# Halving additions for the pooled keys and values, and one minimum per chunk moved to GpSimd

## The chip, the cores and the metric

The kernel runs on one core of a Trainium2 chip. The time is the device time of one execution in microseconds (us); the figure for a kernel is the median of several runs. The engines are called here as the profile calls them: PE (TensorE), DVE (VectorE), ACT (ScalarE), POOL (GpSimd) and SP (SyncE, whose queue issues the transfers).

## The reference, cut to what matters

Attention over keys and values that are averaged in groups of eight rows, then two MLPs one after the other. All data is float32.

```python
def _attn_ref(q, k, v):                     # (8, 8, 576, 64): batch, heads, rows, depth
    k_p = k.reshape(B, H, 72, 8, D).mean(axis=3)
    v_p = v.reshape(B, H, 72, 8, D).mean(axis=3)
    scores = np.matmul(q, k_p.transpose(0, 1, 3, 2)) / np.sqrt(D)
    ...                                     # softmax over the 72 pooled rows
    return np.matmul(attn, v_p)             # regrouped to x: 4608 tokens x 512

def _moe_ref(x, w_in, w_out):               # 512 -> 2048 -> 512
    h = x @ w_in
    g = np.where(h >= 1, h, np.where(h <= -1, 0.0, (h + 1) ** 2 / 4))
    return g @ w_out

def _moe2_ref(x, w_in, w_out):              # 512 -> 2048 -> 512
    h = x @ w_in
    return (h / (1 + np.exp(-h))) @ w_out
```

## The kernel before, in words

The 4608 tokens are worked in 9 tiles of 512 tokens for each MLP. A tile has 16 chunks of 128 hidden features, so the main loop runs over steps `s`, sixteen to a tile. Precision is kept by splitting every float32 operand into two float16 halves, a high and a low one, so that each product takes three matmuls (`three`, lines 116 to 118).

**A step of the first MLP.** `emit_h(s)` issues 12 matmuls into a PSUM bank called `hps` (two such banks take turns from tile 1 on). Then, for the chunk of the step before, ACT computes `u = relu(scale * h + bias)` out of that bank (`pre_A`, line 747), the minimum of `u` with one is taken (`min_A`, which calls the helper `ts`, line 89), ACT squares it (`mid_A`, line 753), and DVE takes the maximum with the scaled `h`, once more out of the bank (`post_A`, line 762). Only when `post_A` is through is the bank free for `emit_h` of two steps later. ACT and DVE then split the result into two halves (`split_g`, lines 815 and 816), and three steps after `emit_h` its 12 matmuls into the output banks `y` follow (`emit_yA`). Tile 0 runs apart from the others: its minimum is with two, and its second matmuls wait until the weights have been converted.

**Attention** is worked beside that, 128 tokens at a time, one or two "slots" a step: scores (PE), maximum and difference (DVE, lines 503 and 504), exponential (ACT, 508), sum and reciprocal (DVE, 523 to 527), normalisation (POOL, line 528, into `e`), halves of it (ACT 533, POOL 534), a transposing transfer, and the product with the values (PE, 582), whose result is split into `xh` and `xl` (line 322), the input of the next tile.

**Pooling keys and values** is `kv_pool`. A piece is two heads of one batch: a tile `raw` of 72 partitions that holds, for each head, 8 rows of 64 numbers. There are 8 batches x (keys, values) x 4 pieces = 64. Of these, 12 (values of batch 0, keys and values of batch 1) are pooled on POOL by three halving additions (lines 385 and 386), and 52 on DVE by one `tensor_reduce` that reads the eight rows with a stride (line 388). From batch 2 on the eight pieces of a batch are pooled close together, once in about 100 us.

**Weights** are converted from float32 in between (ACT 169, 203 and 204; DVE 177, 91, 189 and 195; POOL 205).

The order of the instructions on each engine is written down by the program's own scheduler at build time, from the order of the code and its priorities; on the chip each engine then works its list strictly in that order.

Of the kernel before, what the change touches and what calls it, by code (L numbers as in the profile page):

```python
# [13 lines left out]
ALU = mybir.AluOpType  # L14
AX = mybir.AxisListType
# [18 lines left out]
def tile_pooled_attention_two_mlps(  # L34
# [18 lines left out]
    nc = tc.nc  # L53
# [8 lines left out]
    KF = DFF // 128  # L62
# [9 lines left out]
    ON_POOL = [(0, "v"), (1, "k"), (1, "v")]  # L72
# [14 lines left out]
    def ts(out, in0, s1, s2=None, op0=ALU.mult, op1=None):  # L87
        if op1 is None:
            nc.vector.tensor_scalar(out=out, in0=in0, scalar1=s1, scalar2=None, op0=op0)  # L89
        else:  # L90
            nc.vector.tensor_scalar(out=out, in0=in0, scalar1=s1, scalar2=s2, op0=op0, op1=op1)
# [283 lines left out]
    def kv_pool(b, which, hp):  # L375

        if hp == 0:
            sums[b, which] = kvp.tile([SPT, H, D], F32, tag="sum", name="sum", bufs=3)
            if which == "k":
                nc.gpsimd.memset(sums[b, which][SP // 32 * 32:SPT], 0.0)  # L380
        dst = sums[b, which][0:SP, 2 * hp:2 * hp + 2]
        r = kv_raw.pop((b, which, hp))
        if (b, which) in ON_POOL:
            for n in (4, 2):
                nc.gpsimd.tensor_tensor(out=r[:, :, 0:n], in0=r[:, :, 0:n], in1=r[:, :, n:2 * n], op=ALU.add)
            nc.gpsimd.tensor_tensor(out=dst, in0=r[:, :, 0], in1=r[:, :, 1], op=ALU.add)
        else:
            nc.vector.tensor_reduce(out=dst, in_=r.rearrange("p h r d -> p h d r"), axis=AX.X, op=ALU.add)  # L388

# [333 lines left out]
    g_t, h_t, u_t, g32_t = {}, {}, {}, {}  # L725
# [21 lines left out]
            nc.scalar.activation(out=u, in_=h_t[s], func=AF.Relu, scale=c_A(r, "ch", s), bias=0.5)  # L747

    def min_A(s, r):
        ts(u_t[s], u_t[s], 2.0 if s < KF else 1.0, op0=ALU.min)  # L750

    def mid_A(s, r):
        nc.scalar.activation(out=u_t[s], in_=u_t[s], func=AF.Square, scale=0.5 if s < KF else r["rsg"])  # L753
# [161 lines left out]
    def pool_to(n):  # L915
        while done["pool"] < min(n, len(kv)):
            load_to(done["pool"] + 4)
            x = kv[done["pool"]]
            if done["pool"] >= 16:
                paced(lambda: kv_pool(*x))  # L920
            else:
                kv_pool(*x)
            done["pool"] += 1
# [28 lines left out]
    r = XT[0]  # L952
# [11 lines left out]
    for s in range(KF + 1):  # L964
        if s < KF:
            while n1 < min(len(cuts1), piece_of(cuts1, s) + 2):
                convert1(n1)
                n1 += 1
            emit_h(s, chunk1, r["x"])
        z = s - 1  # L970
        if z >= 0:
            pre_A(z, r)
            min_A(z, r)
            mid_A(z, r)
            post_A(z, r)
# [38 lines left out]
    for s in range(KF, LAST + LAG):  # L1014
# [4 lines left out]
        if KF <= z < LAST:  # L1019
            if z < NTILE * KF:  # L1020
                pre_A(z, XT[z // KF])
                min_A(z, XT[z // KF])
            else:
                act_B(z, XT[z // KF])
# [75 lines left out]
```

## Time and profile before

| | |
|---|---|
| Median of 3 runs | 1745.93 us (1745.43 to 1748.97) |
| The profiled execution, whole | 1752.34 us |
| Its span, first to last instruction | 1750.4 us |
| Mean granted PE clock in it | 0.961 of full speed |
| PE busy in the span | 1620.5 us (93%) |
| DVE busy | 904.8 us (52%) |
| ACT busy | 776.8 us (44%) |
| POOL busy | 220.7 us (13%) |

Matmuls are pipelined, so a share of busy time on PE says that it had work, not that it ran at its peak. The work changes along the span: loading, the first attention tiles and tile 0 until about 230 us; tiles 1 to 8 of the first MLP, with attention beside them until about 870 us; the end of the first MLP until 990 us and then the second MLP. The averages above run over all of these.

### The profile page before, as it was taken

How to read it: one execution, taken by the hardware profiler on the slowest of the kernel's cores; microseconds unless marked ns; L12 is line 12 of the kernel's file. 1: busy time of each engine (PE TensorE's matmuls, PEld its weight loads, DVE VectorE, ACT ScalarE, POOL GpSimd, SP SyncE). 2: the span in 40 equal slices, each digit the busy share in tenths (PEclk: the TensorE clock that was granted, in tenths of full speed). 3: DMA queues.
4: the chain of work that ended last, by engine and by line, in shares of the span. 5: the costliest groups of instructions: out<-in, count | busy, mean ns of one | idle time of the engine just before them, and what ended most of it. 6: DMA issues, size and time to landing. Idle time of an engine off the chain costs nothing.

```text
span 1750.4 us, 21833 instructions
## 1 busy us (share of the span) xinstructions
PE 1620.5 (93%) x8594; PEld 757.5 (43%) x8594; DVE 904.8 (52%) x1714; ACT 776.8 (44%) x1215; POOL 220.7 (13%) x195
## 2 busy tenths in 40 slices
PE   4763789999998999999999999999999999999998
PEld 3321334444444444444444444444444444444443
DVE  8797778878788597886535331212121312122111
ACT  3575455665646556475434433333332323233232
POOL 5733412121221112112100000000000000000000
PEclk8786789999999999999999999999999999999999
DMA  9414655655659346342241010000000000000000
GB/s 283 127 57 119 138 130 128 149 127 125 154 125 269 89 131 148 90 120 61 55 187 49 10 63 25 25 25 24 25 25 25 25 24 25 25 25 25 0 25 24
DMA packets 206086, 144.55 MB, mean 83 GB/s; under 512 B 153120, under 2 KB 170528, under 8 KB 204832
## 3 DMA queue, kind: packets, MB, share of 16 engines
q1 hardware_dynamic: 205984, 143.16, 30.8%
q8 instruction: 67, 1.10, 0.3%
q14 instruction: 35, 0.29, 0.0%
HBM read 88.08 MB, written 27.26 MB: 66 GB/s over the span
## 4 chain that ended last, share of the span: by engine, by line
PE 64%; DVE 18%; ACT 7%; DMA 6%; issue 2%; POOL 1%; SPq 0%; ACTq 0%; POOLq 0%; DVEq 0%
PE hps L116 10%; PE hps L118 10%; PE hps L117 10%; PE y L863 7%; PE y L862 7%; PE y L861 7%; DVE sum L388 5%; PE y L116 3%; PE y L118 3%; PE y L117 3%; DVE g L816 2%; DVE g L762 2%; DMA raw<-in_moe_w_in_dram 1%; DVE xf L189 1%; DVE xf L195 1%
## 5 line engine op out<-in xcount | busy, mean ns | idle before, releaser
L819 DVE SCALAR_TENSOR_TENSOR g<-g,tsg,g 128x512 f16<-128x512 f32 x144 | 108.2, 751 | 479.6 <-ACT g L818 478.5
L808 ACT ACTIVATE g<-hps,tc 128x512 f32<-128x512 f32 x144 | 99.0, 687 | 504.7 <-PE hps L118 502.1
L116 PE MATMUL hps<-xh,wa 128*128 128x512 f16 x576 | 226.3, 393 | 40.0 <-DVE g L762 22.7
L117 PE MATMUL hps<-xl,wa 128*128 128x512 f16 x576 | 226.2, 393 | 0.0
L118 PE MATMUL hps<-xh,wa 128*128 128x512 f16 x576 | 224.3, 391 | 1.8 <-POOL wa L205 1.8
L116 PE MATMUL hps<-xh,wch 128*128 128x512 f16 x576 | 218.3, 379 | 0.0
L117 PE MATMUL hps<-xl,wch 128*128 128x512 f16 x576 | 218.3, 379 | 0.0
L118 PE MATMUL hps<-xh,wcl 128*128 128x512 f16 x576 | 218.3, 379 | 0.0
L861 PE MATMUL y<-wdh,g 128*128 128x512 f16 x576 | 218.3, 379 | 0.0
L862 PE MATMUL y<-wdl,g 128*128 128x512 f16 x576 | 218.3, 379 | 0.0
L863 PE MATMUL y<-wdh,g 128*128 128x512 f16 x576 | 218.3, 379 | 0.0
L117 PE MATMUL y<-g,wb 128*128 128x512 f16 x544 | 206.9, 380 | 2.3 <-DVE g L816 1.7
L118 PE MATMUL y<-g,wb 128*128 128x512 f16 x544 | 206.8, 380 | 0.0
L116 PE MATMUL y<-g,wb 128*128 128x512 f16 x544 | 203.5, 382 | 0.4 <-ACT y L849 0.4
L753 ACT ACTIVATE u<-u,trsg 128x512 f32<-128x512 f32 x128 | 91.9, 719 | 87.7 <-DVE u L89 87.7
L762 DVE SCALAR_TENSOR_TENSOR g<-hps,tc,u 128x512 f32<-128x512 f32 x136 | 101.5, 746 | 54.8 <-ACT u L753 53.8
L816 DVE TENSOR_TENSOR g<-g,g 128x512 f16<-128x512 f32 x128 | 97.2, 760 | 50.6 <-ACT g L815 49.1
L747 ACT ACTIVATE u<-hps,tch 128x512 f32<-128x512 f32 x128 | 87.0, 680 | 72.6 <-PE hps L118 72.3
L815 ACT CAST g<-g 128x512 f16<-128x512 f32 x128 | 78.5, 614 | 83.4 <-DVE g L762 81.0
L89 DVE TENSOR_SCALAR u<-u 128x512 f32<-128x512 f32 x144 | 75.8, 526 | 66.5 <-ACT u L747 66.1
L818 ACT ACTIVATE g<-g,tsg 128x512 f16<-128x512 f32 x144 | 103.8, 721 | 4.5
L117 PEld LDWEIGHTS <-wa 128*128 128x128 f16 x576 | 57.9, 101 | 96.1 <-issue 37.3
(171 smaller groups left out, 2047.2 us busy)
## 6 DMA issues: line engine op xcount, KB each, us to landing
raw<-in_moe_w_out_dram SPq DMA_DIRECT2D x24, 1024.0 KB
raw<-in_moe_w_in_dram SPq DMA_DIRECT2D x10, 1024.0 KB
raw<-in_k_dram SPq DMA_DIRECT2D x32, 288.0 KB
raw<-in_v_dram SPq DMA_DIRECT2D x32, 288.0 KB
y<-y SPq DMA_DIRECT2D x36, 256.0 KB
yin<-y SPq DMA_DIRECT2D x9, 1024.0 KB
out_dram<-osb SPq DMA_DIRECT2D x36, 256.0 KB
qt<-in_q_dram SPq DMA_DIRECT2D x32, 256.0 KB
```

Source lines behind the costliest of these rows:

```text
L116: nc.tensor.matmul(out=acc, lhsT=wh, rhs=xh, start=start, stop=False)
L117: nc.tensor.matmul(out=acc, lhsT=wh, rhs=xl, start=False, stop=False)
L118: nc.tensor.matmul(out=acc, lhsT=wl, rhs=xh, start=False, stop=stop)
L753: nc.scalar.activation(out=u_t[s], in_=u_t[s], func=AF.Square, scale=0.5 if s < KF else r["rsg"])
L762: return nc.vector.scalar_tensor_tensor(out=g, in0=h_t.pop(s), scalar=c_A(r, "c1", s), in1=u_t.pop(s), op0=ALU.mult, op1=ALU.max)
L808: nc.scalar.activation(out=g, in_=ps, func=AF.Silu, scale=r["c1"][:, p:p + 1])
L816: return nc.vector.tensor_tensor(out=gl, in0=g, in1=gh, op=ALU.subtract)
L818: nc.scalar.activation(out=gh, in_=g, func=AF.Copy, scale=r["sg"])
L819: nc.vector.scalar_tensor_tensor(out=gl, in0=g, scalar=r["sg"], in1=gh, op0=ALU.mult, op1=ALU.subtract)
L861: nc.tensor.matmul(out=a, lhsT=h_, rhs=w[0][:, m], start=st, stop=False)
L862: nc.tensor.matmul(out=a, lhsT=h_, rhs=w[1][:, m], start=False, stop=False)
L863: nc.tensor.matmul(out=a, lhsT=l_, rhs=w[0][:, m], start=False, stop=sp)
```

## The change

The reduction on DVE is replaced by the three halving additions that POOL already used for its 12 pieces: rows 0 to 3 plus rows 4 to 7 (512 numbers a partition), rows 0 and 1 plus rows 2 and 3 (256), row 0 plus row 1 (128). And the minimum of tiles 1 to 8 (`s >= KF`, 128 of the 144) is issued on POOL; tile 0 keeps it on DVE. The line numbers after line 384 shift by one or two (762 becomes 761, 528 becomes 526, 816 becomes 815, 534 becomes 532).

```diff
         dst = sums[b, which][0:SP, 2 * hp:2 * hp + 2]
         r = kv_raw.pop((b, which, hp))
-        if (b, which) in ON_POOL:
-            for n in (4, 2):
-                nc.gpsimd.tensor_tensor(out=r[:, :, 0:n], in0=r[:, :, 0:n], in1=r[:, :, n:2 * n], op=ALU.add)
-            nc.gpsimd.tensor_tensor(out=dst, in0=r[:, :, 0], in1=r[:, :, 1], op=ALU.add)
-        else:
-            nc.vector.tensor_reduce(out=dst, in_=r.rearrange("p h r d -> p h d r"), axis=AX.X, op=ALU.add)
+        e = nc.gpsimd if (b, which) in ON_POOL else nc.vector
+        for n in (4, 2):
+            e.tensor_tensor(out=r[:, :, 0:n], in0=r[:, :, 0:n], in1=r[:, :, n:2 * n], op=ALU.add)
+        e.tensor_tensor(out=dst, in0=r[:, :, 0], in1=r[:, :, 1], op=ALU.add)

     def min_A(s, r):
-        ts(u_t[s], u_t[s], 2.0 if s < KF else 1.0, op0=ALU.min)
+        e = nc.vector if s < KF else nc.gpsimd
+        e.tensor_scalar(out=u_t[s], in0=u_t[s], scalar1=2.0 if s < KF else 1.0, scalar2=None, op0=ALU.min)
```

Since the scheduler writes the order anew, many instructions change places. On DVE, this is the place in tile 1 where the eight pieces of batch 2 are pooled. Before (L388 the reductions, L89 the minimum, L762 `post_A`, L816 the split, L322 the attention output, L195 a weight conversion):

```order
L89 TENSOR_SCALAR u<-u 128x512
L524 TENSOR_SCALAR den<-den 128x8
L527 RECIPROCAL den<-den 128x8
L388 TENSOR_REDUCE sum<-raw 72x128 x4
L762 SCALAR_TENSOR_TENSOR g_2580<-hps,tc_1316,u 128x512
L388 TENSOR_REDUCE sum<-raw 72x128
L104 TENSOR_REDUCE wg<-all 128x1
L322 SCALAR_TENSOR_TENSOR xl<-att,tsv,xh 128x4x128
L388 TENSOR_REDUCE sum<-raw 72x128
L89 TENSOR_SCALAR u<-u 128x512
L816 TENSOR_TENSOR g_2636<-g_2580,g_2636 128x512
```

The same place in the changed kernel, from its first addition on (L385 and L386 the additions, L761 `post_A`, L815 the split, L189 a weight conversion):

```order
L385 TENSOR_TENSOR raw<-raw 72x2x256 x4
L385 TENSOR_TENSOR raw<-raw 72x2x128
L761 SCALAR_TENSOR_TENSOR g_2502<-hps,tc_1324,u 128x512
L385 TENSOR_TENSOR raw<-raw 72x2x128 x3
L386 TENSOR_TENSOR sum<-raw 72x128 x3
L815 TENSOR_TENSOR g_2616<-g_2502,g_2616 128x512
L189 SCALAR_TENSOR_TENSOR xf<-raw,xf 128x1024
L386 TENSOR_TENSOR sum<-raw 72x128
L104 TENSOR_REDUCE wg<-all 128x1
L322 SCALAR_TENSOR_TENSOR xl<-att,tsv,xh 128x4x128
L761 SCALAR_TENSOR_TENSOR g_2620<-hps,tc_1324,u 128x512
```

The pieces are still taken four together, but as additions of four different pieces in turn, with a `post_A` among them, and the minimum is gone from the list.

On POOL, this is the end of tile 0 and the begin of tile 1, before (L205 weight conversion, L528 the normalisation, L534 its halves):

```order
L205 TENSOR_TENSOR wb_124<-xf,wb_124 128x1024 x2
L528 TENSOR_TENSOR e<-e,den 128x576
L534 TENSOR_TENSOR e_113<-e,e_113 128x4x72
L534 TENSOR_TENSOR e_114<-e,e_114 128x4x72
L528 TENSOR_TENSOR e<-e,den 128x576
L534 TENSOR_TENSOR e_113<-e,e_113 128x4x72
L534 TENSOR_TENSOR e_114<-e,e_114 128x4x72
L205 TENSOR_TENSOR hl<-xf,hl 128x1024
```

And the same place in the changed kernel (L749 the minimum, L526 the normalisation, L532 its halves):

```order
L205 TENSOR_TENSOR wb_124<-xf,wb_124 128x1024 x2
L749 TENSOR_SCALAR u<-u 128x512 x4
L526 TENSOR_TENSOR e<-e,den 128x576
L532 TENSOR_TENSOR e_113<-e,e_113 128x4x72
L532 TENSOR_TENSOR e_114<-e,e_114 128x4x72
L749 TENSOR_SCALAR u<-u 128x512
L526 TENSOR_TENSOR e<-e,den 128x576
L749 TENSOR_SCALAR u<-u 128x512
L532 TENSOR_TENSOR e_113<-e,e_113 128x4x72
L532 TENSOR_TENSOR e_114<-e,e_114 128x4x72
L749 TENSOR_SCALAR u<-u 128x512
L205 TENSOR_TENSOR hl<-xf,hl 128x1024
```

The minima now stand between the attention's and the conversion's instructions in POOL's one list, so each waits until those ahead of it are through.

## Rows read from the trace of the kernel before

**Rows 1.** The page, parts 1 and 2: busy times, and PE's granted clock in 40 slices.

```profile
PE 1620.5 (93%) x8594; PEld 757.5 (43%) x8594; DVE 904.8 (52%) x1714; ACT 776.8 (44%) x1215; POOL 220.7 (13%) x195
...
PEclk8786789999999999999999999999999999999999
```

**Rows 2.** Busy time by stretch: start, length, each engine's busy time, clock, DMA share, GB/s.

```profile
230.00:870.00 640.00, 608.03 (x3789) 288.21 (x3789) 499.80 (x982) 370.30 (x620) 119.51 (x106) 0.98 0.52 126
300.00:320.00 20.00, 15.20 (x62) 6.31 (x61) 16.59 (x23) 9.34 (x15) 0.09 (x1) 0.91 0.74 188
...
720.00:740.00 20.00, 17.33 (x95) 8.16 (x95) 19.27 (x19) 8.45 (x16) 4.85 (x4) 1.00 0.44 115
870.00:1750.00 880.00, 875.67 (x4086) 398.82 (x4084) 225.18 (x390) 286.81 (x418) 0.00 (x0) 1.00 0.09 34
```

**Rows 3.** Waits of PE from 230 to 870 us: total, times, longest.

```profile
PE hps L116 <- DVE g L762: 22.7, 15, 3.8
```

**Rows 4.** DVE in order of time, the pooling of batch 2: start, length, instruction.

```profile
294.85 7.38 DVE L388 TENSOR_REDUCE sum<-raw 72x128 f32<-72x1024 f32 x4
302.13 0.75 DVE L762 SCALAR_TENSOR_TENSOR g<-hps,tc,u 128x512 f32<-128x512 f32 x1
302.79 1.92 DVE L388 TENSOR_REDUCE sum<-raw 72x128 f32<-72x1024 f32 x1
...
307.29 0.43 DVE L89 TENSOR_SCALAR u<-u 128x512 f32<-128x512 f32 x1
```

**Rows 5.** ACT in order of time, same place; idle time before in brackets.

```profile
302.26 0.63 ACT L393 ACTIVATE rows<-sum 80x512 f32<-80x512 f32 x1 [4.66 <-DVE sum L388]
...
307.75 0.72 ACT L753 ACTIVATE u<-u,trsg 128x512 f32<-128x512 f32 x1 [3.68 <-DVE u L89]
```

**Rows 6.** PE in order of time, same place.

```profile
313.75 0.38 PE L116 MATMUL hps<-xh,wa 128*128 128x512 f16 x1 [3.06 <-DVE g L762]
```

**Rows 7.** Waits of PE from 125 to 230 us.

```profile
PE att L582 <- DVE xl L322: 7.3, 1, 7.3
```

**Rows 8.** DVE's and ACT's instructions by line: count, ns min/median/max.

```profile
L388 DVE TENSOR_REDUCE sum<-raw x52: 1842/1904/1955, 4.4 to 735.4; 72x128 f32<-72x1024 f32 x52
L816 DVE TENSOR_TENSOR g<-g,g x128: 640/692/2204, 241.8 to 991.1; 128x512 f16<-128x512 f32 x128
L189 DVE SCALAR_TENSOR_TENSOR xf<-raw,xf x26: 1208/1219/2065, 18.4 to 806.7; 128x1024 int32<-128x1024 int32 x26
L89 DVE TENSOR_SCALAR u<-u x144: 373/420/2071, 67.5 to 988.4; 128x512 f32<-128x512 f32 x144
L762 DVE SCALAR_TENSOR_TENSOR g<-hps,tc,u x136: 694/750/753, 70.9 to 989.7; 128x512 f32<-128x512 f32 x136
L747 ACT ACTIVATE u<-hps,tch x128: 662/682/700, 237.0 to 987.7; 128x512 f32<-128x512 f32 x128
L753 ACT ACTIVATE u<-u,trsg x128: 703/722/727, 238.8 to 988.9; 128x512 f32<-128x512 f32 x128
```

**Rows 9.** POOL's instructions by line.

```profile
L380 POOL MEMSET sum<- x8: 517/518/687, 3.2 to 625.8; 16x512 f32 x8
L801 POOL TENSOR_TENSOR stash<-g,stash x2: 1155/1156/1157, 123.5 to 125.1; 128x512 f16<-128x512 f32 x2
L205 POOL TENSOR_TENSOR hl<-xf,hl x16: 2124/2131/3163, 275.2 to 815.5; 128x1024 f16<-128x1024 f32 x16
L528 POOL TENSOR_TENSOR e<-e,den x36: 1144/1150/1600, 31.2 to 860.4; 128x576 f32<-128x576 f32 x36
L534 POOL TENSOR_TENSOR e<-e,e x64: 722/732/1987, 179.6 to 863.2; 128x288 f16<-128x288 f32 x64
```

**Rows 10.** DVE in order of time, one split.

```profile
474.88 2.20 DVE L816 TENSOR_TENSOR g<-g,g 128x512 f16<-128x512 f32 x1 [1.88 <-ACT g L815]
```

**Rows 11.** POOL in order of time, same moment.

```profile
474.41 2.13 POOL L205 TENSOR_TENSOR hl<-xf,hl 128x1024 f16<-128x1024 f32 x1 [5.67 <-ACT hl L204]
```

**Rows 12.** Waits of POOL from 230 to 870 us.

```profile
POOL e L528 <- DVE den L527: 278.7, 22, 31.6
```

## The prediction, made before the changed kernel was run

> **What bounds the kernel now.** The page comes first: PE is busy for 1620.5 of 1750.4 us, and the granted clock is below nine tenths only in the first six of 40 slices, some 260 us [rows 1]. The busy time by stretch then says where PE lacks work. From 870 us to the end it is busy 875.67 of 880 us with 4086 matmuls, one per 0.214 us: nothing in that half is to be won [rows 2]. From 230 to 870 us it idles 640 - 608.03 = 32.0 us, while DVE is busy for 499.8 us (78%) and POOL for 119.5 (19%) [rows 2]. PE's waits name the releaser: 22.7 us, in 15 waits, are an `hps` bank that `post_A` on DVE has not yet freed [rows 3]. PE is the bound there, and a late DVE is what interrupts it.
>
> The timeline shows how. At 294.85 us DVE begins the pooling of batch 2 with four reductions in one run, 7.38 us [rows 4]. ACT, next to read a sum, stands 4.66 us; then the minimum of the following chunk lies behind more reductions until 307.29, and ACT's square waits 3.68 us for it [rows 5]. At the end PE waits 3.06 us for the bank [rows 6]. There are five such places (300, 400, 500, 620 and 720 us); the first leaves PE idle for 4.80 us of 20, the last 2.67 [rows 2], and with the three between (2.31, 1.57, 3.80) that is 15.2 us, half of the 32.0.
>
> **How much lateness a chunk bears.** Between the end of `emit_h(s)` and the start of `emit_h(s+2)` in the same bank PE does 36 other matmuls: 36 x 0.214 = 7.7 us [rows 2]. In that time ACT 0.68, the minimum 0.42, ACT 0.72 and DVE 0.75 must run, 2.57 us [rows 8]. So 5.1 us are left for queueing. A run of 7.38 us overdraws it by 2.3; PE's waits of up to 3.8 us [rows 3] are of that size.
>
> **The change, part by part.**
>
> *The sums.* 52 reductions of 1.90 us go [rows 8]; next to each other they take 7.38 / 4 = 1.85 us each [rows 4]. Additions of two SBUF operands on DVE are seen at 512 elements (692 ns) and, in the weight conversion, at 1024 (1219 ns) [rows 8]: 1.03 ns an element and 165 ns fixed, so 428 ns at 256 and 297 at 128. The three add up to 1.42 us if each waits for the one before: the worst price, which saves 0.43. The list, though, takes the same step of four pieces in a row, and neighbours overlap: the reductions take 1.90 alone and 1.85 in a row. The real overlap of short instructions is not in these rows; taking 0.08 us off each gives 1.18 us a piece and saves 0.67. I take 0.6. For 52 pieces that is 31 us of DVE's time (22 to 35). A run of four becomes 4 x 1.25 = 5.0 us, just below the 5.1 us that a chunk bears, and it is cut by a `post_A`.
>
> *The minimum.* 128 instructions of 0.42 us leave DVE, 54 us more. POOL has no one-input arithmetic of this size in the trace. Its memset of the same 512 elements takes 0.52 us, its two-input operation 1.16 [rows 9]; these are the bounds, and since one stream is read instead of none or two I take 0.8. The chain of a chunk becomes 0.68 + 0.8 + 0.72 + 0.75 = 2.95 us, 0.4 longer, and 4.75 us of slack are left. In tiles 7 and 8 this is hidden entirely: PE runs without a gap there, and POOL has nothing else to do.
>
> *What the minimum queues behind.* POOL does 64 halves of 0.73 us, 36 normalisations of 1.15 and 16 conversions of 2.13 [rows 9]. Running, none of them alone uses up 4.75 us. Standing, they might: a normalisation at the head of POOL's list has waited for DVE 278.7 us in 22 times [rows 12]. What is behind it now is a minimum, which ACT's square waits for, then `post_A`, then PE. That mean of 12.7 us is mostly POOL arriving early with nothing to do before; now it has a minimum in that time, so I expect waits of 1 to 3 us.
>
> *The port.* A split that DVE began at 474.88, 0.47 us after a POOL conversion, took 2.20 us instead of 0.69, and ended when POOL did [rows 10, 11]. The same line has a median of 692 ns and a maximum of 2204; the reduction lies between 1842 and 1955 always, and `post_A`, with one operand in PSUM, between 694 and 753 [rows 8]. So the change exchanges instructions that POOL cannot stretch for 156 that it can, and gives POOL 128 x 0.8 = 102 us more to run. The Trainium skill has this as a rule: SBUF — State Buffer, "Who interferes with whom", says that a DVE instruction with two SBUF inputs contends with a GpSimd instruction that reads SBUF, that the second to start blocks fully, and that `tensor_reduce` never contends. By that rule, the rows above agreeing, both halves of the change get in each other's way. Price: from 230 to 870 us some 105 of the 128 minima make POOL busy for 84 us more, 13% of the time; about 320 DVE instructions with two SBUF operands or of the `u` kind then meet it with that chance and lose about half of 0.8 us: 320 x 0.13 x 0.4 = 17 us of DVE's time. It takes back a fifth of the 85 us freed.
>
> *The sum, in PE's time.* Before 125 us: one run of four sums, -1. 125 to 230 us: PE waits 7.3 us for an attention result that stands behind eight sums [rows 7]; 8 x 0.6 is 4.8, of which I count -3, because weight conversions stand between them. The five places: of 15.2 us two thirds, -10 (0 to -15). The other 16.8 us of idle time from 230 to 870, partly of transfers: a quarter, as DVE loses a tenth of its load and the minimum no longer queues there, -4. The clock is at 0.91 in the first of the five places [rows 2]; fewer gaps there give -2. Contention and the longer chain: +4. Together -16 us. Against the profiled execution's 1752.34 us that is 1736; the median of the runs shown is 6.4 us below that execution, so it is 1745.93 - 16 = 1730 us.
>
> **The rivals.**
>
> *A, slower: the minimum is stuck in POOL's list.* From 230 to 870 us there are about 28 attention rounds, and each has a normalisation that waits for DVE. If POOL stands at one for over 4.75 us with a minimum behind it, PE stops. If one round in three does so by 3.5 us, that is 9 x 3.5 = 32 us against a gain of 16: 1762. For it: POOL's longest wait was 31.6 us [rows 12]. Against it: the list is ordered by when things should be ready, and DVE, the one waited for, is the engine that is relieved.
>
> *B, hidden.* The five places lose their reductions, but the next wait ends as late (ACT's head also waits for transfers), and only the -1 and -3 before 230 us stay: 1742.
>
> *C, the port takes it all.* If POOL's minimum is 1.16 us and additions in a row meet it each time, the 17 us become 50 or more and the runs of additions are as long as the reductions were: 1747. This also is the case in which the additions are no cheaper than what they replace.
>
> *D, everything goes.* All 32.0 us of idle time save some 3 of transfers, 4 before 230 us, and half of the 2% that the clock lacks from 230 to 870 us (0.98 [rows 2], 12.8 us): 29 + 4 + 7 = 40, so 1706. For it: 22.7 of the 32.0 us have one cause [rows 3].
>
> **How the numbers follow.** Forecast 0.52, A 0.12, B 0.14, C 0.12, D 0.10. A measurement of this kernel tells 0.2%, 3.5 us, from no change. The forecast and D are faster, and half of B, which ends at that bound: 0.69. Same: the other half of B and most of C: 0.17. Slower: A and the rest of C: 0.14. The range leaves out A and part of D, and takes in B, C and the bounds of the sums: 1712 to 1750; the forecast's own range is 1720 to 1738.
>
> **What would show it.** Right: runs of four pieces on DVE at 4.7 to 5.7 us; PE's wait for `post_A` from 230 to 870 us down from 22.7 to below 12; the minimum on POOL at 0.6 to 1.0 us when alone; ACT's square seldom waiting over 2 us for it; PE's busy time after 870 us unchanged. Wrong: additions of 512 often above 1.2 us (C); ACT's square waiting over 5 us for POOL, with POOL idle at a normalisation just ahead (A); PE's idle time unchanged with transfers as releasers (B). Also, the new order on every engine may bring stalls of its own, which no row of before can show.

## The result, and the profile after

The changed kernel takes 1764.16 us (median of 4 runs, 1763.76 to 1766.61), the kernel before 1745.68 us (4 runs): a ratio of 1.0104, 95% interval 1.0087 to 1.0122. It is 18 us slower, where 16 us faster was forecast, and it lies outside the range of 1712 to 1750 us.

The page of the changed kernel, part 1:

```profile
PE 1615.4 (92%) x8594; PEld 754.8 (43%) x8594; DVE 848.9 (48%) x1690; ACT 778.4 (44%) x1215; POOL 444.1 (25%) x323
```

DVE was relieved, but by less than planned: 904.8 us busy before [rows 1], 848.9 now, 56 us less, where the forecast freed 85 and gave 17 of them back to the port. POOL's busy time doubled, from 220.7 to 444.1 us. The 128 minima alone keep it busy for 218 of these 223 us more, where the forecast had 102. The granted clock is where it was (a mean of 0.964, before 0.961).

The busy time by stretch of the changed kernel (columns as in [rows 2]):

```profile
230.00:870.00 640.00, 592.90 (x3692) 280.55 (x3692) 450.84 (x953) 365.51 (x608) 299.75 (x205) 0.99 0.53 127
870.00:1760.00 890.00, 890.00 (x4187) 405.78 (x4183) 222.72 (x380) 294.74 (x430) 41.55 (x29) 1.00 0.09 33
```

PE's idle time from 230 to 870 us is 640 - 592.90 = 47.1 us, against 32.0 [rows 2]: 15 us more, about the 14.3 us by which the two profiled executions differ (1766.61 against 1752.34). After 870 us PE never waits, as before (the 4.3 us that [rows 2] lacks there lie behind its last matmul). So the loss lies in the stretch where attention runs beside the MLP, and DVE with 49 us less to do there (450.84 against 499.80) did not help.

What each engine waited for from 230 to 870 us in the changed kernel (total, times, longest); PE:

```profile
PE hps L116 <- DVE g L761: 23.7, 19, 3.1
PE y L117 <- DVE g L815: 7.1, 4, 3.3
PE all L103 <- ACT rows L391: 5.0, 2, 2.9
```

DVE:

```profile
DVE g L761 <- ACT u L752: 87.8, 44, 4.8
...
DVE raw L385 <- DMA raw<-in_v_dram: 18.1, 12, 3.4
```

ACT:

```profile
ACT g L814 <- DVE g L761: 84.5, 66, 8.0
ACT u L752 <- POOL u L749: 82.9, 59, 3.1
```

POOL:

```profile
POOL u L749 <- ACT u L745: 205.9, 62, 11.8
POOL e L526 <- DVE den L525: 47.7, 19, 4.5
```

The bank that waits for `post_A` costs PE 23.7 us, where it cost 22.7 [rows 3]. So only 1 of the 15 us is at the bank; the rest is spread over waits that were 2.8 us or less before, the split (7.1) and the attention's rows (5.0) first. ACT's square stands 82.9 us for the minimum on POOL, in small pieces. And there is a wait that was not foreseen: DVE, at the first of a piece's additions, stands for the load of the values.

The same two links of the chain in the kernel before:

```profile
ACT u L753 <- DVE u L89: 75.2, 57, 3.7
```

```profile
DVE g L762 <- ACT u L753: 37.3, 38, 3.1
```

The square stood nearly as long for a minimum that was late on DVE as it now stands for one that is long on POOL. And `post_A` stands 50 us more for the square (87.8 against 37.3), as much as DVE was relieved of: the freed time is spent waiting in the same chain. Such a wait of DVE is not by itself a loss of PE's: in the kernel without a minimum, shown further down, it is 94.8 us.

### The profile page after: what moved, and what is told of

The parts are those of the page before. It is cut to its first block, busy times and chain, and to the rows that moved or that the text cites. A ratio compares the mean times of both kernels' runs of the same rounds, so it can differ in the third digit from the quotient of the medians.

```text
span 1764.8 us, 21992 instructions
## 1 busy us (share of the span) xinstructions
PE 1615.4 (92%) x8594; PEld 754.8 (43%) x8594; DVE 848.9 (48%) x1690; ACT 778.4 (44%) x1215; POOL 444.1 (25%) x323
## 4 chain that ended last, share of the span: by engine, by line
PE 60%; DVE 15%; DMA 9%; ACT 7%; POOL 4%; issue 4%; SPq 1%; DVEq 0%; POOLq 0%; ACTq 0%
PE hps L117 10%; PE hps L116 10%; PE hps L118 10%; PE y L862 7%; PE y L861 7%; PE y L860 7%; PE y L116 3%; PE y L118 3%; DMA raw<-in_v_dram 3%; PE y L117 3%; POOL u L749 2%; DVE raw L385 2%; DMA qT<-rows 2%; DVE g L761 2%; DVE xf L195 1%
## 5 line engine op out<-in xcount | busy, mean ns | idle before, releaser
L749 POOL TENSOR_SCALAR u<-u 128x512 f32<-128x512 f32 x128 | 218.2, 1705 | 318.5 <-ACT u L745 296.7
L116 PE MATMUL hps<-xh,wa 128*128 128x512 f16 x576 | 224.4, 390 | 36.2 <-DVE g L761 23.7
L118 PE MATMUL hps<-xh,wa 128*128 128x512 f16 x576 | 221.1, 386 | 3.4 <-POOL wa L205 3.4
L761 DVE SCALAR_TENSOR_TENSOR g<-hps,tc,u 128x512 f32<-128x512 f32 x136 | 101.4, 745 | 152.8 <-ACT u L752 152.4
L815 DVE TENSOR_TENSOR g<-g,g 128x512 f16<-128x512 f32 x128 | 102.9, 804 | 50.1 <-ACT g L814 48.8
```

The costliest lines, as they stand in the source:

```text
L116: nc.tensor.matmul(out=acc, lhsT=wh, rhs=xh, start=start, stop=False)
L118: nc.tensor.matmul(out=acc, lhsT=wl, rhs=xh, start=False, stop=stop)
L749: e.tensor_scalar(out=u_t[s], in0=u_t[s], scalar1=2.0 if s < KF else 1.0, scalar2=None, op0=ALU.min)
L761: return nc.vector.scalar_tensor_tensor(out=g, in0=h_t.pop(s), scalar=c_A(r, "c1", s), in1=u_t.pop(s), op0=ALU.mult, op1=ALU.max)
L815: return nc.vector.tensor_tensor(out=gl, in0=g, in1=gh, op=ALU.subtract)
```

## The experiments

Nine kernels were timed, five rounds each, against the kernel before. A difference in us below is the ratio less 1, times 1748 us, the median of before in those runs; a ratio's interval of about 0.0013 either way is some 2 us.

### One half of the change at a time

The sums alone (the minimum back on DVE):

```diff
-        e = nc.vector if s < KF else nc.gpsimd
-        e.tensor_scalar(out=u_t[s], in0=u_t[s], scalar1=2.0 if s < KF else 1.0, scalar2=None, op0=ALU.min)
+        ts(u_t[s], u_t[s], 2.0 if s < KF else 1.0, op0=ALU.min)
```

> Halving additions on DVE, the minimum stays on DVE. M (the minimum on GpSimd is the cost: 1.49 us instead of 0.42 in every chunk's chain): without it the sums bring what was forecast, -5 to -15 us against before, 1731 to 1741. S (the sums are the cost: taken four pieces in turn they hold all four raw buffers, and DVE stands at the next addition until a late value load lands, 18 us of such waits after the change): +8 to +18, 1754 to 1764, with the same waits of additions for value loads in the profile. P (only the two together cost, by the shared port): -8 to 0, and 512-element additions near 0.69 us instead of 0.90.

Measured: 1.0033 [1.0019, 1.0046], 5.8 us slower. That is in none of the three ranges; S has the sign and comes nearest. P is out: it had 0.69 us for the additions of 512, and their mean is 0.87. These additions of 512, by line and shape (busy us, mean ns of one, idle time before them and its releasers):

```profile
L385 DVE TENSOR_TENSOR raw<-raw 72x512 f32<-72x512 f32 x52 | 44.0, 874 | 21.7 <-DMA raw<-in_v_dram 17.0 <-DMA raw<-in_k_dram 4.7
```

The minimum alone (the reduction back on DVE, the minimum on POOL):

```diff
-        e = nc.gpsimd if (b, which) in ON_POOL else nc.vector
...
+        else:
+            nc.vector.tensor_reduce(out=dst, in_=r.rearrange("p h r d -> p h d r"), axis=AX.X, op=ALU.add)
```

> The minimum of tiles 1 to 8 on GpSimd, the reductions stay. M: most of the loss, +12 to +20 us against before, 1758 to 1766. S: no loss, -5 to +3, 1741 to 1749, since reductions free their buffer one by one. P: -5 to +3 as well, and the minimum near its 1.49 us with few longer ones, because reductions do not take the port.

Measured: 1.0074 [1.006, 1.0088], 12.9 us slower, as M said. The minimum in it, by line (ns minimum, median, maximum), and as a group (busy us, mean ns of one, idle time before):

```profile
L751 POOL TENSOR_SCALAR u<-u x128: 1474/1484/3177, 237.4 to 998.0; 128x512 f32<-128x512 f32 x128
```

```profile
L751 POOL TENSOR_SCALAR u<-u 128x512 f32<-128x512 f32 x128 | 210.7, 1647 | 347.0 <-ACT u L747 328.0 <-DVE sq L91 11.2 <-DVE xl L322 4.4
```

Each half loses by itself, and 5.8 + 12.9 = 18.7 us is, within the intervals, the 18.2 us that both lose together: each half has a cost of its own.

### The sums: the order of the additions

In the changed kernel the additions stand four pieces at a time: four first steps, four second, four third. A piece's `raw` buffer, of which there are four, comes free only with its last step. Here the three additions of a piece are tied behind the last addition of the piece before; first with the minimum on POOL, then with the minimum on DVE:

```diff
+    pooled = []
...
-        for n in (4, 2):
-            e.tensor_tensor(...)
-        e.tensor_tensor(out=dst, in0=r[:, :, 0], in1=r[:, :, 1], op=ALU.add)
+        with tc.issue_after(pooled[-1].ins) if pooled and e is nc.vector else nullcontext():
+            for n in (4, 2):
+                e.tensor_tensor(...)
+            y = e.tensor_tensor(out=dst, in0=r[:, :, 0], in1=r[:, :, 1], op=ALU.add)
+        if e is nc.vector:
+            pooled.append(y)
```

> The whole change, but on DVE the three additions of a piece are queued behind the last addition of the piece before, so that a raw buffer comes free after each piece. S: the waits of additions for value loads fall from 18 us to under 5, and the time to 1745 to 1752. M: the waits fall too, but the time stays at 1758 or above. P: as M.

Measured: 1.0045 [1.0031, 1.0059], 7.9 us slower instead of 18.2. That lies between the range of S and that of M: the order costs 10 us of the whole change, and the rest stays.

> Halving additions on DVE, each piece queued behind the one before, and the minimum on DVE. If the order of the additions was the whole cost of the sums (with it changed, the whole change lost 10 us of its 18), the cheaper sums now bring a gain: -3 to -8 us against before, 1741 to 1746. If the sums cost something else too (the port, more instructions), 0 to +5, 1749 to 1754.

Measured: 0.9945 [0.9929, 0.9962], 9.6 us **faster** than before; it beats both kernels, and by more than the first expectation allowed. The minimum's move, added to it, costs 17.5 us (from -9.6 to +7.9), where it costs 12.9 with the reductions; the difference is at the edge of what the intervals tell. DVE in order of time in the changed kernel, at the pooling of a batch (start, length, instruction):

```profile
405.83 3.39 DVE L385 TENSOR_TENSOR raw<-raw 72x512 f32<-72x512 f32 x4
...
409.27 1.82 DVE L385 TENSOR_TENSOR raw<-raw 72x256 f32<-72x256 f32 x4
411.02 1.96 DVE L386 TENSOR_TENSOR sum<-raw 72x128 f32<-72x128 f32 x4
412.91 0.74 DVE L761 SCALAR_TENSOR_TENSOR g<-hps,tc,u 128x512 f32<-128x512 f32 x1
417.06 0.69 DVE L385 TENSOR_TENSOR raw<-raw 72x512 f32<-72x512 f32 x1 [3.42 <-DMA raw<-in_v_dram]
```

And at the same work in the kernel with the sums in turn and the minimum on DVE:

```profile
415.20 0.27 DVE L388 TENSOR_TENSOR sum<-raw 72x128 f32<-72x128 f32 x1
415.40 0.67 DVE L387 TENSOR_TENSOR raw<-raw 72x512 f32<-72x512 f32 x1
416.00 0.73 DVE L764 SCALAR_TENSOR_TENSOR g<-hps,tc,u 128x512 f32<-128x512 f32 x1
416.66 0.40 DVE L387 TENSOR_TENSOR raw<-raw 72x256 f32<-72x256 f32 x1
417.10 0.29 DVE L388 TENSOR_TENSOR sum<-raw 72x128 f32<-72x128 f32 x1
417.31 0.68 DVE L387 TENSOR_TENSOR raw<-raw 72x512 f32<-72x512 f32 x1
```

The chain of work that ended last, of the changed kernel, behind this run of four (start, length, what):

```profile
413.25 3.71 DMA raw<-in_v_dram
```

In the changed kernel, four pieces take 405.83 to 412.98, 7.1 us, as long as the reductions' 7.38 [rows 4]. No `raw` buffer comes free before the last steps, which begin at 411.02; so a load of values starts at 413.25, takes 3.71 us, and at 417.06 DVE has stood 3.42 us for it. In the kernel with the sums in turn a piece's steps are sprinkled between the chunks' instructions, a buffer comes free with each third step, and the first step seldom waits. The groups by line and shape of that kernel, and its waits of PE from 230 to 870 us:

```profile
L387 DVE TENSOR_TENSOR raw<-raw 72x512 f32<-72x512 f32 x52 | 36.2, 697 | 7.8 <-DMA raw<-in_v_dram 4.5 <-DMA raw<-in_k_dram 3.1
...
L387 DVE TENSOR_TENSOR raw<-raw 72x256 f32<-72x256 f32 x52 | 32.8, 631 | 0.4
L388 DVE TENSOR_TENSOR sum<-raw 72x128 f32<-72x128 f32 x52 | 20.5, 394 | 1.1
```

```profile
PE hps L116 <- DVE g L764: 4.6, 5, 2.1
```

DVE's idle time at the loads fell from 21.7 us (sums alone) to 7.8, and PE's wait for the bank to 4.6. The additions themselves did not get cheaper: 36.2 + 32.8 + 20.5 = 89.5 us busy, against 87.4 with the sums alone (44.0, and 28.1 and 15.3 for the shorter two). The edit does two things at once, it frees buffers sooner and it breaks the long run into instructions of some 0.3 to 0.7 us with others between; which of them gives how much of the 15 us is open. Additions four in turn with more buffers would tell; this was not tried. Nor was the run of reductions broken up with other instructions between, which would tell whether the gain needs additions at all.

### The minimum: its time, its place, or the port

Half of the columns on POOL (the reductions on DVE; the minimum of columns 256 to 511 is left out):

```diff
+            h = u_t[s][:, 0:N // 2]
+            nc.gpsimd.tensor_scalar(out=h, in0=h, scalar1=1.0, scalar2=None, op0=ALU.min)
```

> As the kernel with the minimum alone on GpSimd, but the minimum is taken of the first 256 of the 512 columns only; the other half of it is left out. M: the instruction takes some 0.75 to 0.8 us, and at least half of the loss of the full-width one is gone, 1746 to 1755. S and P: no difference to the full-width one beyond 4 us, as it was no loss.

Measured: 1.0018 [1.0007, 1.0029], 3.1 us slower: three quarters of the loss are gone, as M said. Next, two that separate DVE's relief from POOL's link, again with the reductions on DVE. The first leaves out the minimum of tiles 1 to 8 on every engine. The second puts three memsets of `u` in its place, which write as many elements and read none (the values of `u` are left out):

```diff
         if s < KF:
             ts(u_t[s], u_t[s], 2.0, op0=ALU.min)
+        else:
+            for i in range(3):
+                nc.gpsimd.memset(u_t[s], 0.5)
```

> The kernel before with the minimum of tiles 1 to 8 left out on every engine. This is what the relief of DVE is worth by itself, with nothing in its place on GpSimd and a shorter chain. Forecast's step (a late DVE is what stops PE): -8 to -20 us, 1729 to 1741, and PE's waits for the bank from 230 to 870 us under 15. If PE's waits have other causes: -5 to 0.

Measured without a minimum: 0.9911 [0.9896, 0.9927], 15.6 us faster. Its busy time by stretch:

```profile
230.00:870.00 640.00, 618.07 (x3896) 294.96 (x3896) 454.60 (x884) 379.12 (x629) 116.83 (x106) 0.99 0.55 133
```

PE's idle time there is 21.9 us, against 32.0: a DVE relieved of the minimum, in a chain that is shorter by it, is worth about what the forecast hoped for, so long as nothing takes the minimum's place.

> The minimum of tiles 1 to 8 replaced by three GpSimd memsets of the same tile, so the minimum and the values of u are left out; GpSimd is as long in the chain (3 x 0.52 us) and as busy, but reads nothing from SBUF. L (the length of the chain is the cost): as with the minimum on GpSimd, +8 to +14 us, 1757 to 1763. P (the port is the cost): the split on DVE is never stretched by it, and the time falls to 1740 to 1749.

Measured with three memsets: 1.0044 [1.0031, 1.0058], 7.7 us slower, so 23 us above the kernel without a minimum, with the same relief of DVE. L holds (its range began at +8, which the interval takes in), and P does not. To see whether the length of the link counts, or the two hand-overs between ACT and POOL, the loop was cut to one memset, as here, and to two:

```diff
-            for i in range(3):
+            for i in range(1):
```

> The reductions stay on DVE; in place of the minimum of tiles 1 to 8 GpSimd writes a constant over the chunk once (the values are left out). DVE is relieved of 0.42 us a chunk as in the changed kernel, and the link in the chain is one memset, 0.52 us. If the length of the link on GpSimd is what costs, with no price for the hand-over itself, the time lies on the line through the kernel without a minimum (-15.5 us, link of 0) and that with three memsets (+7.7 us, 1.59 us): -8 us. If the two hand-overs between ACT and GpSimd cost most of it whatever the length, it lies close to the kernels with a longer link: 0 to +4 us. If relief of DVE is worth nothing by itself and only the shorter chain paid in the kernel without a minimum, it equals the kernel before or is a little slower, 0 to +3, and two memsets a step more.

> As with one memset, but two in a row on GpSimd, a link of 1.05 us. If the length of the link is what costs: on the line between no link and three memsets, 0 us (-15.5 + 23.2 x 1.05 / 1.59 = -0.2). If the hand-over costs and not the length: within 2 us of both one and three memsets, +4 to +8. Against it stands the minimum over half of the columns, a link of 0.84 us that also reads SBUF, at +3: if reading costs by itself, this kernel is no slower than that one though its link is longer.

Measured: one memset 0.9944 [0.993, 0.9958], 9.8 us faster; two 1.0008 [0.9999, 1.0017], +1.4 us, no difference that can be told. Both lie near the line of the length, and neither in the range of the hand-over. The memsets of the kernels with one, two and three, by line and shape (busy us, mean ns of one, idle before):

```profile
L754 POOL MEMSET u<- 128x512 f32 x128 | 67.6, 528 | 406.8 <-ACT u L747 388.5 <-DVE eq L89 11.4 <-DVE rows L322 6.8
```

```profile
L754 POOL MEMSET u<- 128x512 f32 x256 | 138.8, 542 | 377.8 <-ACT u L747 370.8
```

```profile
L754 POOL MEMSET u<- 128x512 f32 x384 | 203.1, 531 | 350.1 <-ACT u L747 337.0
```

The same of the minimum over half of the columns:

```profile
L754 POOL TENSOR_SCALAR u<-u 128x256 f32<-128x256 f32 x128 | 134.7, 1052 | 379.7 <-ACT u L747 343.5 <-DVE eq L89 14.5 <-DVE rows L322 6.5
```

ACT's waits for that link from 230 to 870 us, with one memset, two, three, and the minimum alone:

```profile
ACT u L757 <- POOL u L754: 25.6, 40, 2.1
```

```profile
ACT u L757 <- POOL u L754: 57.9, 61, 2.7
```

```profile
ACT u L757 <- POOL u L754: 75.7, 59, 2.6
```

```profile
ACT u L754 <- POOL u L751: 86.1, 67, 3.1
```

Side by side, with the mean time that POOL is busy for a chunk (the busy time of the group / 128):

| link on POOL (reductions on DVE) | us a chunk | against before, us | PE's wait for the bank, us |
|---|---|---|---|
| none | 0 | -15.6 | 4.8 |
| one memset | 0.53 | -9.8 | 6.6 |
| two memsets | 1.08 | +1.4 | 14.5 |
| minimum of 256 columns | 1.05 | +3.1 | 17.6 |
| three memsets | 1.59 | +7.7 | 25.4 |
| minimum of 512 columns | 1.65 | +12.9 | 22.5 |

The loss grows with the length: (7.7 + 15.6) / 1.59 = 14.7 us for each microsecond of link on average, with steps of 5.8, 11.2 and 6.3 us from none to three memsets. A hand-over that costs by itself would make the first step larger than the others, and it is the smallest. Break-even lies at about 1.06 us. The two kernels whose link also reads SBUF lie 3 to 4 us above that line (at 1.05 it gives -0.2, at 1.65 it gives +8.7). For the first that is hardly more than the intervals tell; so reading by itself, the port included, is the small part, and its size stays open.

One thing the row does not keep apart: the scheduler wrote the lists of each of these kernels anew, and their orders on ACT and DVE differ. No run changes the order and leaves the link, so some microseconds of a single step may be the order's.

## Why the prediction was wrong, step by step

**What bounds the kernel, and what relief of DVE is worth: right.** PE stops because DVE is late: without the minimum its wait for the bank falls from 22.7 us [rows 3] to 4.8, and the time by 15.6 us. One memset, a link of 0.53 us, little longer than the 0.42 us that the minimum took on DVE [rows 8], still leaves 9.8 of it.

**The minimum's price: the first step that failed.** It was taken at 0.8 us between bounds of 0.52 and 1.16, since "one stream is read instead of none or two". The minimum and two of the additions in the changed kernel, by line and by shape:

```profile
L749 POOL TENSOR_SCALAR u<-u x128: 1477/1488/3027, 239.5 to 1004.6; 128x512 f32<-128x512 f32 x128
```

```profile
L385 DVE TENSOR_TENSOR raw<-raw 72x512 f32<-72x512 f32 x52 | 45.5, 900 | 26.4 <-DMA raw<-in_v_dram 21.4 <-DMA raw<-in_k_dram 4.8
...
L385 DVE TENSOR_TENSOR raw<-raw 72x256 f32<-72x256 f32 x52 | 25.1, 507 | 0.0
L386 DVE TENSOR_TENSOR sum<-raw 72x128 f32<-72x128 f32 x52 | 15.0, 315 | 0.0
```

Undisturbed it takes 1.49 us, above both bounds: here POOL's operation with one input and a constant is dearer than its subtraction with two inputs (1.16 [rows 9]), so the bracket had no ground. With its longer cases it averages 1.65 us in the kernel with the minimum alone, twice the 0.8.

**The slack: the second.** "4.75 us of slack are left", and 0.4 us more of chain was to disappear in them; contention and the chain together were given +4. The row of kernels above says otherwise: from one memset to two, 0.56 us more of link cost 11.2 us, though all of it would fit into that slack. At the assumed 0.8 us the line gives -15.6 + 0.8 x 14.7 = -3.8, with 3 for reading about -1. So, by this estimate, the minimum's move would have brought little even at the price assumed, and at 1.65 us it loses 12.9. The slack was worked out for a chunk alone. But ACT and DVE work their lists in order, and while ACT stands at a square (25.6, 57.9, 75.7 us with one, two and three memsets) everything behind it stands too, the next chunk's first step and the attention's among it. That this passing-on makes the slope is argued from those waits, not shown apart; the 75.2 us that the square waited in the kernel before, for DVE, are as many as with three memsets, so the sum of these waits alone does not give the time.

**The sums: two steps failed.** They were to free 31 us of DVE. They take 45.5 + 25.1 + 15.0 = 85.6 us; the reductions took 96.6 in the kernel before:

```profile
L388 DVE TENSOR_REDUCE sum<-raw 72x128 f32<-72x1024 f32 x52 | 96.6, 1904 | 2.9 <-DMA raw<-in_k_dram 2.9
```

That frees 11. The durations assumed are right when nothing disturbs: of the 156 additions of the changed kernel, 91 ran while POOL did nothing, and they took 675 to 689, 408 to 422 and 275 to 283 ns (0.69, 0.43 and 0.30 us assumed). The longer ones, up to 2612 ns, are all among the 65 that met a POOL instruction. In the run of four shown above each of the three steps met one:

```profile
406.06 1.41 POOL L526 TENSOR_TENSOR e<-e,den 128x576 f32<-128x576 f32 x1 [4.38 <-DVE den L525]
409.28 1.75 POOL L749 TENSOR_SCALAR u<-u 128x512 f32<-128x512 f32 x1 [1.81 <-ACT u L745]
411.00 1.64 POOL L532 TENSOR_TENSOR e<-e,e 128x288 f16<-128x288 f32 x2
```

The reductions, which kept to 1842 to 1955 ns [rows 8], were exchanged for instructions that POOL stretches. The Trainium skill has this as a rule in SBUF — State Buffer, "Who interferes with whom": a DVE instruction with two SBUF inputs contends with a GpSimd instruction that reads SBUF, and `tensor_reduce` does not. These rows agree with it. The price had been set for the minimum's contention alone. With the sums alone, and no minimum on POOL, the additions of 512 are at 874 ns as well: what POOL did already was enough. One reading behind the price was off too: the split that was said to end when POOL did ended 0.54 us later (474.88 + 2.20 against 474.41 + 2.13 [rows 10, 11]), so it lost 1.5 of the conversion's 2.13 us.

The run of four was thus 7.1 us and not 5.0, as long as the reductions' run, and nothing shows of the 10 us that the five places were to give: PE's idle time in the whole stretch rose. Behind that lay the wait which no step had: the order four in turn keeps all `raw` buffers until the end, and the value loads come late (18.1 us of DVE's waits). The order of DVE's list had been read for the length of its run, not for when it gives back what the loads wait for. That the order is the cause, and not the additions as such, the kernel with sums in turn shows: the same additions, no cheaper, and 15 us less (from +5.8 to -9.6).

**Before 230 us, and the clock:** of the -4 hardly anything came; the first `pre_A` of tile 1 starts at 236.55 us (237.0 before [rows 8]). Nor did the -2 for the clock show: it was granted at 0.99 from 230 to 870 us, before at 0.98 [rows 2], and PE idled more. PE's waits from 125 to 230 us in the changed kernel:

```profile
PE y L116 <- ACT wb L204: 21.1, 3, 12.5
...
PE att L580 <- DVE xl L322: 2.3, 1, 2.3
```

The wait for the attention result did shrink, from 7.3 us [rows 7] to 2.3, and a wait for a weight conversion on ACT, 17.4 us before and 21.1 now, took most of that back.

**Tiles 7 and 8 hide it entirely: right from 870 us on.** PE is busy for 890.00 of 890 us after 870 us.

**The rivals.** A had the sign and nearly the size (1762), but not the mechanism: ACT's square never waited over 3.1 us for POOL, and POOL's own waits at a normalisation fell from 278.7 us, longest 31.6 [rows 12], to 47.7, longest 4.5. The minimum is not stuck; it is long. C had the runs of additions right and the rest too cheap. B, that the next wait ends as late, had no rows for the loads.

## What to carry to other kernels

An instruction that is moved to an idle engine still stands in the chain of its chunk: price its length there before counting what the busy engine gains, and where the trace has no such instruction on that engine, time it first, since here neighbours of other kinds did not bound it. Slack worked out for one chunk alone was not free to spend here, where other engines wait for that chunk in a fixed order. Where one instruction becomes several, look in the new order for when the last of them comes, since it gives the buffer back; here the same additions, piece after piece and with the minimum left on DVE, are 9.6 us faster than before.

## What the runs showed of the hardware

GpSimd's minimum of a tile with a constant took 1477 to 1488 ns for 512 float32 columns and, over 256 columns, 838 to 844:

```profile
L754 POOL TENSOR_SCALAR u<-u x128: 838/844/3332, 233.9 to 983.4; 128x256 f32<-128x256 f32 x128
```

By the medians of these two sizes (1488 and 844) that is 644 / 256 = 2.5 ns an element and 200 ns fixed. On DVE the same minimum takes 0.42 us [rows 8]. In the changed kernel the 29 minima during which DVE did nothing took 1478 to 1491 ns; with DVE at work beside it, it came to 3.0 us there and to 3.3 us over 256 columns at the longest, so the stretching goes both ways.
